# An FFT long convolution feeding an ELU MLP: batches transformed one by one instead of in pairs

## The chip, the cores and the metric

The kernel runs on one core of a Trainium2 chip. The metric is the device time of one execution in microseconds (us). TensorE (PE) does the matmuls, ScalarE (ACT) copies and activations, VectorE (DVE) and GpSimd (POOL) the elementwise work, and the SyncE queue (SP) issues nearly all DMAs.

## The reference

For four batches of 12480 positions by 128 channels, the first part is a gated long convolution, the second an MLP over all 49920 rows:

```python
h_filt = (np.maximum(pos_emb @ w1, 0.0) @ w2) * np.exp(-0.01 * pos)[:, None]
u = x * v
y = irfft(rfft(u, 2S) * rfft(h_filt, 2S)[None])[:, :S, :]    # causal convolution
a = (x * y).reshape(B * S, D)
h = a @ w_in                                                   # 128 -> 2048
g = np.where(h > 0.0, h, np.exp(np.minimum(h, 0.0)) - 1.0)     # ELU
return g @ w_out                                               # 2048 -> 128
```

## The kernel before

The sequence of one batch is laid out as 2 halves (w) x 104 rows x 60 columns (n). The convolution is done by a two-stage transform. Stage 1 (`stage1`) loads x and v, multiplies them (`gate`, on POOL), splits the product into a high and a low part (`split`), multiplies by 104x104 matrices (tiles aps) and stores the result to DRAM (`a_d`). Stage 2 (`stage2`) loads 104 slices k, multiplies each by a 120x120 matrix from a table (`forward`, tiles xps), multiplies by the filter's spectrum on DVE (tiles p), adds on POOL, transforms back (`inverse`, tiles bps) and stores to DRAM (`b_d`). Every product is three matmuls of high and low parts (`mm3`), save those in plain 32-bit.

The MLP (`Mlp.go`) works in blocks of 416 rows. One block loads `b_d` and x, does the last inverse matmuls (`conv_out`, tiles yps), gates, transposes (`transp`), and then takes 8 steps: in each, `up_proj` does six matmuls of 416 columns (tiles fps), ACT computes the exponential (n), DVE the ELU (g), POOL a rounding cast (g_h), DVE the low part (g_l), and `down_proj`, three steps later, six matmuls more (tiles ops).

Batches go in pairs: a tile holds 2 columns n by 2 batches. The order is written out by hand:

1. Stage 1 of pair 0 alone, with the filter's MLP and its transform (class `Filter`: tiles pt, rp, hps, Hps) and the unpacking of the 64-bit weights between its steps, one filter step for each of its 30 groups.
2. Stage 2 of pair 0 alone. Here each k also makes the filter's spectrum (`spectrum`, tiles fps from hl) and stores it to `f_d`.
3. The MLP over pair 0 (60 blocks, 480 steps). After each step the generator of pair 1's transforms (`side`, from `fft1`) is advanced by 0.92 of a step on average; 8 of its steps run before the MLP. Pair 1's stage 2 reads `f_d`.
4. The MLP over pair 1 (480 steps) with no transforms beside it and a third PSUM buffer pair for up_proj (`psf2`).

Pair 0's transforms keep 32-bit tiles in DRAM and split them after loading (`split_a`, `split_b`); pair 1's write the high and low parts already split. Each engine takes its instructions in this written order.

Of the kernel before, what the change touches and what calls it, by code (L numbers as in the profile page):

```python
# [19 lines left out]
TC = 5 * N2 + RI  # L20
G = 2
NG = N2 // G
HB = 2
CH = HB * D
NT = G * HB * N1
TG = 2
DFF = 2048
# [3 lines left out]
NBK = 2 * NG  # L31
FWD = ((0, 1), (2, 0))
# [4 lines left out]
def fftconv_gate_elu_mlp_kernel(ctx: ExitStack, tc: tile.TileContext, x, v, pos_emb, w1, w2,  # L37
# [21 lines left out]

    a_d = [dram.tile([N1, h + 1, 2, N2, 2, CH], F32, name=f"a_d{h}") for h in range(2)]  # L60
    b_d = [dram.tile([N1, 2, h + 1, 2, N2, CH], F32, name=f"b_d{h}") for h in range(2)]
# [17 lines left out]
    def stage1(st, h, ps_pool, ps_tag, first, eng_gate):  # L79
        b0 = h * HB  # L80
        xv = st.enter_context(tc.tile_pool(name=f"xv{h}", bufs=3 if first else 2))
        up = st.enter_context(tc.tile_pool(name=f"up{h}", bufs=2))
        ap = st.enter_context(tc.tile_pool(name=f"ap{h}", bufs=5 if first else 3))
        ld, us = {}, {}

        def load(g):
            if g >= NG:
                return
            xt = xv.tile([N1, 2, HB, G, D], F32, tag="xt", name="xt")
            vt = xv.tile([N1, 2, HB, G, D], F32, tag="vt", name="vt")  # L90
            for w in range(2):
                nc.sync.dma_start(out=xt[:, w], in_=xq[:, w, b0:b0 + HB, g * G:(g + 1) * G, :])
                nc.sync.dma_start(out=vt[:, w], in_=vq[:, w, b0:b0 + HB, g * G:(g + 1) * G, :])
            ld[g] = (xt, vt)

        def gate(g):
            if g >= NG:
                return
            xt, vt = ld[g]
            e = nc.vector if first and g < 2 else eng_gate  # L100
            e.tensor_tensor(out=vt, in0=xt, in1=vt, op=ALU.mult)  # L101

        def split(g):
# [3 lines left out]
            u_h = up.tile([N1, 2, HB, G, D], F32R, tag="u_h", name="u_h")  # L107
            u_l = up.tile([N1, 2, HB, G, D], F32R, tag="u_l", name="u_l")
# [4 lines left out]
        if first:  # L113
            filt = Filter(st)
        for g in range(3 if first else 2):
            if first:
                filt.load(g)
            load(g)
            if first:
                filt.load_w(g)  # L120
        gate(0)
        gate(1)
        if first:
            for q in range(3):
                filt.step(0, q)
        split(0)
        stores = []

        def store():
            if stores:  # L130
                g, r, t = stores.pop()
                nc.sync.dma_start(out=a_d[h][:, :, r, g * G:(g + 1) * G].rearrange("k z n w c -> k z (n w c)"),
                                  in_=t.bitcast(F32).rearrange("k z n w c -> k z (n w c)"))

        for g in range(NG):
            gate(g + 2) if first else None
            u_h, u_l = us.pop(g)
            for i in range(4):
                r, w = divmod(i, 2)
                f = FWD[w][r]  # L140
                if w == 0:
                    a_sb = ap.tile([N1, 1 + h, G, 2, CH], F32R if h else F32, tag="a_sb", name="a_sb")
                ps = ps_pool.tile([N1, 512], F32, tag=ps_tag, name="aps")
                mm3(ps, dft_h[:, f, :], dft_l[:, f, :], u_h[:, w], u_l[:, w])
                dst = [a_sb[:, z, :, w, :].rearrange("p n (b d) -> p b n d", b=HB) for z in range(1 + h)]
                src = ps.rearrange("p (b n d) -> p b n d", b=HB, n=G)
                if first and w == 0:
                    nc.vector.tensor_copy(out=dst[0], in_=src)
                else:
                    copy(dst[0], src)  # L150
                if not first:
                    nc.vector.tensor_tensor(out=dst[1], in0=src, in1=dst[0], op=ALU.subtract)
                if first and i < 3:
                    filt.step(g + 1, i)
# [4 lines left out]
                if i == 0:  # L159
                    if first:  # L160
                        filt.load(g + 3)
                        filt.load_w(g + 3)
                    load(g + (3 if first else 2))
                if i == 1:
                    split(g + 1)
                    if first:
                        filt.split_w(g - 1)
# [3 lines left out]
            if first:  # L171
                filt.transform(g)
                filt.weights(g)
# [5 lines left out]
    class Filter:  # L179
# [3 lines left out]
        def __init__(self, st):  # L183
            c1 = st.enter_context(tc.tile_pool(name="c1", bufs=1))
            self.pp = st.enter_context(tc.tile_pool(name="pp", bufs=3))
# [12 lines left out]
        def load(self, g):  # L198
            if g >= NG:
                return  # L200
            p = self.pp.tile([N1, 2, G, 64], F32, tag="pos", name="pos")
            nc.sync.dma_start(out=p, in_=posq[:, :, g * G:(g + 1) * G, :])
            self.pos[g] = p

        def step(self, g, q):
            if g >= NG:
                return
            hp, psh = self.hp, self.psh
            if q == 0:
                p = self.pos.pop(g)  # L210
                pt = psh.tile([64, 2 * G, N1], F32, tag="h", name="pt")
                for n in range(2 * G):
                    nc.tensor.transpose(out=pt[:, n, :], in_=p[:, n // G, n % G, :], identity=id_sb[:N1, :N1])
                pt_sb = hp.tile([64, 2 * G, N1], F32, tag="pt_sb", name="pt_sb")
                copy(pt_sb, pt)
                self.t[g] = pt_sb
            elif q == 1:
                rp = psh.tile([64, 2 * G, N1], F32, tag="h", name="rp")
                nc.tensor.matmul(out=rp, lhsT=self.w1, rhs=self.t[g], start=True, stop=True)
                r_sb = hp.tile([64, 2 * G, N1], F32, tag="r_sb", name="r_sb")  # L220
                nc.scalar.activation(out=r_sb, in_=rp, func=ACTF.Relu)
                self.t[g] = r_sb
            elif q == 2:
                r_sb = self.t.pop(g)
                hps = psh.tile([N1, 2, G, D], F32, tag="h", name="hps")
                for n in range(2 * G):
                    nc.tensor.matmul(out=hps[:, n // G, n % G, :], lhsT=r_sb[:, n, :], rhs=self.w2,
                                     start=True, stop=True)
                h_sb = hp.tile([N1, 2, G, D], F32, tag="h_sb", name="h_sb")
# [508 lines left out]
```

## Time and profile before

| what | value |
|---|---|
| time, median of 3 runs | 3669.15 us (3665.28 to 3671.24) |
| the profiled execution: time, span | 3675.88 us, 3674.1 us |
| mean granted TensorE clock | 0.967 of full speed |
| busy: PE, DVE, ACT, POOL | 94%, 84%, 66%, 63% of the span |
| DMA: bytes, mean rate | 525.90 MB, 143 GB/s |
| chain that ended last: PE, DVE, DMA | 67%, 10%, 10% of the span |

Busy shares are unions over the span; matmuls overlap one another, so a PE at 94% is not one that could not take more. The four stages have different limits and have to be read one by one.

### The profile page before, as it was taken

How to read it: one execution, taken by the hardware profiler on the slowest of the kernel's cores; microseconds unless marked ns; L12 is line 12 of the kernel's file. 1: busy time of each engine (PE TensorE's matmuls, PEld its weight loads, DVE VectorE, ACT ScalarE, POOL GpSimd, SP SyncE). 2: the span in 40 equal slices, each digit the busy share in tenths (PEclk: the TensorE clock that was granted, in tenths of full speed). 3: DMA queues.
4: the chain of work that ended last, by engine and by line, in shares of the span. 5: the costliest groups of instructions: out<-in, count | busy, mean ns of one | idle time of the engine just before them, and what ended most of it. 6: DMA issues, size and time to landing. Idle time of an engine off the chain costs nothing.

```text
span 3674.1 us, 50190 instructions
## 1 busy us (share of the span) xinstructions
PE 3439.7 (94%) x16780; PEld 2981.2 (81%) x16780; DVE 3098.9 (84%) x3803; ACT 2419.5 (66%) x3238; POOL 2320.9 (63%) x1508
## 2 busy tenths in 40 slices
PE   7887888779998999999999999989999999999999
PEld 4565555468887888888888888879999999999998
DVE  5566999879998998998898898968888888888887
ACT  3344554467886666666676666757777777777776
POOL 2233888747776777777677677645555565655655
PEclk8688999989999999999999999999999999999999
DMA  5687888766676455555555455332222222222220
GB/s 178 194 276 231 255 254 255 230 192 204 209 211 188 134 160 169 158 156 153 156 165 168 135 167 170 107 77 70 57 66 61 60 67 57 70 57 69 58 64 19
DMA packets 352784, 525.90 MB, mean 143 GB/s; under 512 B 24678, under 2 KB 220358, under 8 KB 352526
## 3 DMA queue, kind: packets, MB, share of 16 engines
q1 hardware_dynamic: 352105, 522.52, 48.9%
q8 instruction: 134, 2.20, 0.2%
q14 instruction: 124, 1.02, 0.1%
q10 hardware_dynamic: 421, 0.16, 0.0%
HBM read 318.12 MB, written 204.47 MB: 142 GB/s over the span
## 4 chain that ended last, share of the span: by engine, by line
PE 67%; DVE 10%; DMA 10%; issue 4%; SPq 3%; ACT 3%; POOL 2%; POOLq 0%; DVEq 0%; ACTq 0%
PE ops L52 9%; PE ops L51 9%; PE fps L51 8%; PE fps L52 8%; PE fps L53 8%; PE ops L53 8%; DVE g_l L571 3%; PE bps L428 3%; DMA h_d<-hsb 2%; DMA al<-a_d 2%; PE otp L593 1%; PE yps L52 1%; PE yps L51 1%; PE yps L53 1%; PE xps L51 1%
## 5 line engine op out<-in xcount | busy, mean ns | idle before, releaser
L565 POOL CAST g_h<-g 128x832 fp32r<-128x832 f32 x960 | 1308.9, 1365 | 963.7 <-DVE g L562 947.4
L562 DVE SCALAR_TENSOR_TENSOR g<-n,fps 128x832 f32<-128x832 f32 x960 | 975.6, 1016 | 332.8 <-ACT n L556 328.5
L555 ACT ACTIVATE n<-fps 128x832 f32<-128x832 f32 x960 | 832.1, 867 | 631.4 <-PE fps L53 618.3
L571 DVE TENSOR_TENSOR g_l<-g,g_h 128x832 fp32r<-128x832 f32 x960 | 1113.9, 1160 | 7.7 <-POOL g_h L565 7.7
L556 ACT ACTIVATE n<-n 128x832 f32<-128x832 f32 x960 | 864.7, 901 | 30.5
L51 PE MATMUL fps<-t_h,wi_h 128*128 128x416 f32 x1920 | 722.9, 376 | 20.7 <-DVE g L562 19.5
L52 PE MATMUL ops<-g_l,wo_h 128*128 128x416 f32 x1920 | 685.1, 357 | 28.8 <-DVE g_l L571 28.4
L51 PE MATMUL ops<-g_h,wo_h 128*128 128x416 f32 x1920 | 683.1, 356 | 8.0 <-ACT o_sb L56 0.7
L52 PE MATMUL fps<-t_l,wi_h 128*128 128x416 f32 x1920 | 676.3, 352 | 0.0
L53 PE MATMUL fps<-t_h,wi_l 128*128 128x416 f32 x1920 | 675.8, 352 | 0.0
L53 PE MATMUL ops<-g_h,wo_l 128*128 128x416 f32 x1920 | 675.4, 352 | 0.0
L408 POOL TENSOR_TENSOR p<-p 120x768 f32<-120x768 f32 x206 | 478.1, 2321 | 92.2 <-DVE p L400 48.6
L51 PEld LDWEIGHTS fps<-t_h,wi_h 128*128 128x128 f32 x1920 | 363.2, 189 | 62.5 <-DVE g L562 24.5
L52 PEld LDWEIGHTS ops<-g_l,wo_h 128*128 128x128 f32 x1920 | 362.2, 189 | 61.0 <-DVE g_l L571 57.5
L52 PEld LDWEIGHTS fps<-t_l,wi_h 128*128 128x128 f32 x1920 | 364.9, 190 | 31.2 <-issue 14.2
L51 PEld LDWEIGHTS ops<-g_h,wo_h 128*128 128x128 f32 x1920 | 361.7, 188 | 32.4 <-issue 28.3
L53 PEld LDWEIGHTS fps<-t_h,wi_l 128*128 128x128 f32 x1920 | 362.5, 189 | 3.5
L53 PEld LDWEIGHTS ops<-g_h,wo_l 128*128 128x128 f32 x1920 | 361.8, 188 | 4.0
L101 POOL TENSOR_TENSOR vt<-xt,vt 104x1024 f32<-104x1024 f32 x58 | 145.7, 2512 | 247.6 <-DMA vt<-in_v_dram 216.5
L395 DVE TENSOR_TENSOR p<-xps,f 120x512 f32<-120x512 f32 x416 | 282.4, 679 | 10.2 <-PE xps L53 6.3
L428 PE MATMUL bps<-p,t 120*120 120x512 f32 x416 | 218.1, 605 | 43.8 <-POOL p L409 42.2
L409 POOL TENSOR_TENSOR p<-p 120x256 f32<-120x256 f32 x206 | 235.1, 1141 | 16.1
(100 smaller groups left out, 4428.2 us busy)
## 6 DMA issues: line engine op xcount, KB each, us to landing
a_d<-a_sb SPq DMA_DIRECT2D x60, 832.0 KB
al<-a_d SPq DMA_DIRECT2D x104, 480.0 KB
b_d<-b_sb SPq DMA_DIRECT2D x104, 480.0 KB
b<-b_d SPq DMA_DIRECT2D x60, 832.0 KB
t<-in_tab_dram SPq DMA_DIRECT2D x104, 393.8 KB
xt<-in_x_dram SPq DMA_DIRECT2D x120, 208.0 KB
vt<-in_v_dram SPq DMA_DIRECT2D x120, 208.0 KB
a_d<-a_sb SPq DMA_DIRECT2D x60, 416.0 KB
```

The costliest lines, as they stand in the source:

```text
L51: nc.tensor.matmul(out=ps, lhsT=hi, rhs=bh, start=start, stop=False)
L52: nc.tensor.matmul(out=ps, lhsT=hi, rhs=bl, start=False, stop=False)
L53: nc.tensor.matmul(out=ps, lhsT=lo, rhs=bh, start=False, stop=stop)
L395: nc.vector.tensor_tensor(out=p[:, :2], in0=ps[:, :CH].rearrange("p (u b d) -> p u b d", u=1, b=HB).to_broadcast([RI, 2, HB, D]), in1=f[:, ...
L408: e.tensor_tensor(out=q, in0=q, in1=p, op=ALU.add)
L409: e.tensor_tensor(out=q[:, 1], in0=q[:, 1], in1=q[:, 2], op=ALU.add)
L428: nc.tensor.matmul(out=ps, lhsT=t[:, o, 5 * N2:], rhs=y[:, :2], start=True, stop=True)
L555: nc.scalar.activation(out=n, in_=ps[:, :, :NT], func=ACTF.Relu, scale=-1.0)
L556: nc.scalar.activation(out=n, in_=n, func=ACTF.Exp, scale=-1.0)
L562: nc.vector.scalar_tensor_tensor(out=g, in0=n, scalar=-1.0, in1=ps[:, :, :NT], op0=ALU.add, op1=ALU.max)
L565: nc.gpsimd.tensor_copy(out=g_h, in_=g)
L571: nc.vector.tensor_tensor(out=g_l, in0=g, in1=g_h, op=ALU.subtract)
```

## The change

Batches are transformed one at a time. Stage 1 takes groups of 4 columns n of one batch where it took 2 columns of 2 batches, stage 2 takes two slices k of one batch where it took one slice of two. Only batch 0 is transformed ahead of the MLP. The MLP is one loop over 120 blocks; its side work in quarter p is the transforms of batch p + 1, advanced by 1.04 of a step at each MLP step, and in the last quarter there is none. The filter keeps its groups of 2 columns, so each of its 30 steps now goes beside half a group of stage 1. The stage 2 table loses its duplicated columns (420 to 300); ahead of the MLP, POOL copies the columns that `spectrum` needs twice into a tile td.

The core of the diff:

```diff
-TC = 5 * N2 + RI
-G = 2
+TC = 3 * N2 + RI
+G = 4
+GF = 2
+SHARE = 1.04
...  stage1: the filter's steps, two for each group g of four
-                if first and i < 3:
-                    filt.step(g + 1, i)
+                if first:
+                    q = 2 * g + r
+                    filt.step(q + 1, 2 * w)
                 ps = ps_pool.tile([N1, 512], F32, tag=ps_tag, name="aps")
                 mm3(ps, dft_h[:, f, :], dft_l[:, f, :], u_h[:, w], u_l[:, w])
...
+                    if w == 0:
+                        filt.step(q + 1, 1)
+                        filt.load(q + 4)
+                        filt.load_w(q + 4)
+                    else:
+                        filt.transform(q)
+                        filt.weights(q)
+                        filt.split_w(q - 1)
...  stage2
-        d = 4 if first else 3
+        d = 3 if first else 2
...  split_t
-            th = tp.tile([RI, TG, 4 * N2], F32R, tag="th", name="th")
-            tl = tp.tile([RI, TG, 4 * N2], F32R, tag="tl", name="tl")
+            th = tp.tile([RI, TG, 3 * N2], F32R, tag="th", name="th")
+            tl = tp.tile([RI, TG, 3 * N2], F32R, tag="tl", name="tl")
...
+            if first:
+                td = tp.tile([RI, TG, 2, 2, N2], F32, tag="td", name="td")
+                for r in range(2):
+                    v = t[:, :, (1 + r) * N2:(2 + r) * N2].rearrange("p o (u n) -> p o u n", u=1)
+                    nc.gpsimd.tensor_copy(out=td[:, :, r], in_=v.to_broadcast([RI, TG, 2, N2]))
...  forward
-            ps = ps_pool.tile([RI, 2 * CH], F32, tag=ps_tag, name="xps")
-            mm3(ps, th[:, o, c:c + RI], tl[:, o, c:c + RI], a_h, a_l)
+            ps = ps_pool.tile([RI, TG, 2, D], F32, tag=ps_tag, name="xps")
+            for o in range(TG):
+                mm3(ps[:, o].rearrange("p w d -> p (w d)"), th[:, o, c:c + RI], tl[:, o, c:c + RI], a_h[:, o], a_l[:, o])
...  stage2's loop: inverse one turn behind, where it was two
-            split_a(k + 2)
-            inverse(k - 2)
-            yield
+            inverse(g - 1)
             yield
...  Mlp
-            blocks = [(w, n) for w in range(2) for n in range(NG)]
+            blocks = [(b, w, n) for b in range(NB) for w in range(2) for n in range(NG)]
+            ALL = len(blocks)
...
+                if s == (NB - 1) * per:
+                    psf2 = alone()
...
-                while side is not None and done < (s + 1) * share:
+                p, q = divmod(s, per)
+                if q == 0:
+                    done = 0
+                while p in side and done < (q + 1) * SHARE:
                     done += 1
-                    if next(side, None) is END:
-                        side = None
+                    if next(side[p], None) is END:
+                        del side[p]
...
-                    if c == 0:
-                        split_b(j + 2)
                     if c == 1:
                         conv_out(j + 1)
                         load(j + 3)
+                    if c == 2:
+                        split_b(j + 2)
...
-            run = mlp.run(sx, 0)
-            next(run)
-            side = fft1(psx)
-            for _ in range(8):
-                next(side)
-            side = run.send((side, 0.92))
+        side = {p: fft(p + 1, psx) for p in range(NB - 1)}
+        mlp.run(side, alone)
```

On PE in stage 1 ahead of the MLP, one turn of the filter stood among twelve matmuls of 512 columns (pt, rp, hps are the filter's MLP, aps is stage 1; the transform Hps follows):

```order
L213 MATMUL pt<-id_sb,pos 64x104 x4
L51 MATMUL aps<-u_h,dft_h 104x512
L52 MATMUL aps<-u_l,dft_h 104x512
L53 MATMUL aps<-u_h,dft_l 104x512
L219 MATMUL rp<-pt_sb,w_sb 64x416
L51 MATMUL aps<-u_h,dft_h 104x512
L52 MATMUL aps<-u_l,dft_h 104x512
L53 MATMUL aps<-u_h,dft_l 104x512
L227 MATMUL hps<-w_sb,r_sb 104x128 x4
L51 MATMUL aps<-u_h,dft_h 104x512
L52 MATMUL aps<-u_l,dft_h 104x512
L53 MATMUL aps<-u_h,dft_l 104x512
```

The same turn now, up to the first matmuls of Hps:

```order
L217 MATMUL pt<-id_sb,pos 64x104 x4
L53 MATMUL aps<-u_h,dft_h 104x512
L54 MATMUL aps<-u_l,dft_h 104x512
L55 MATMUL aps<-u_h,dft_l 104x512
L223 MATMUL rp<-pt_sb,w_sb 64x416
L231 MATMUL hps<-w_sb,r_sb 104x128 x4
L53 MATMUL aps<-u_h,dft_h 104x512
L54 MATMUL aps<-u_l,dft_h 104x512
L55 MATMUL aps<-u_h,dft_l 104x512
L53 MATMUL Hps<-h_h,dft_h 104x256
L54 MATMUL Hps<-h_l,dft_h 104x256
L55 MATMUL Hps<-h_h,dft_l 104x256
```

Two aps triples stand beside a filter turn where four stood, and rp and hps are neighbours.

On PE in stage 2 ahead of the MLP, from one inverse (bps) to the next, before (one k of two batches; fps is the spectrum, xps the forward transform):

```order
L428 MATMUL bps<-p,t 120x512
L380 MATMUL fps<-hl,t 120x256 x2
L51 MATMUL xps<-a_h,th 120x512
L52 MATMUL xps<-a_l,th 120x512
L53 MATMUL xps<-a_h,tl 120x512
L51 MATMUL xps<-a_h,th 120x512
L52 MATMUL xps<-a_l,th 120x512
L53 MATMUL xps<-a_h,tl 120x512
```

Now (two k of one batch), the first half; six more xps rows follow before the next bps:

```order
L439 MATMUL bps<-p,t 120x256 x2
L395 MATMUL fps<-hl,td 120x256 x4
L53 MATMUL xps<-a_h,th 120x256
L54 MATMUL xps<-a_l,th 120x256
L55 MATMUL xps<-a_h,tl 120x256
L53 MATMUL xps<-a_h,th 120x256
L54 MATMUL xps<-a_l,th 120x256
L55 MATMUL xps<-a_h,tl 120x256
```

One turn keeps the columns of forward and inverse and has twice the spectrum; there are 52 turns where there were 104.

On SP at the start of the MLP, before (xt and vt are loads of pair 1's stage 1, a_d_58 its stores; b and x are the loads of the MLP's first blocks):

```order
L93 DMA vt<-in_v_dram 104x2x256
L132 DMA a_d_58<-a_sb 208x1x1024 x2
L92 DMA xt<-in_x_dram 104x2x256
L93 DMA vt<-in_v_dram 104x2x256
L92 DMA xt<-in_x_dram 104x2x256
L93 DMA vt<-in_v_dram 104x2x256
L132 DMA a_d_58<-a_sb 208x1x1024
L499 DMA b_6834<-b_d_59 104x2x512
L501 DMA x_6835<-in_x_dram 104x2x256
```

Now, from the last stores of stage 2 on:

```order
L429 DMA b_d_61<-b_sb 120x2x256 x2
L504 DMA b_5089<-b_d_61 104x8x128
L505 DMA x_5088<-in_x_dram 104x512
L504 DMA b_5094<-b_d_61 104x8x128
L505 DMA x_5093<-in_x_dram 104x512
L504 DMA b_5121<-b_d_61 104x8x128
L505 DMA x_5120<-in_x_dram 104x512
L93 DMA xt<-in_x_dram 104x2x512
L94 DMA vt<-in_v_dram 104x2x512
```

The MLP's loads come first and the next batch's transform starts behind them, inside the loop.

## Rows read from the trace of the kernel before

**Rows 1.** Busy time by stage: stretch, length, PE, PEld, DVE, ACT, POOL, PEclk, DMA share, GB/s

```profile
0.00:334.00 334.00, 264.81 (x1140) 180.22 (x1140) 188.45 (x344) 131.60 (x230) 83.49 (x48) 0.81 0.69 222
334.00:717.00 383.00, 338.75 (x1243) 221.71 (x1244) 364.04 (x569) 192.82 (x360) 318.99 (x205) 1.00 0.79 248
717.00:766.00 49.00, 19.00 (x40) 8.80 (x38) 16.63 (x20) 11.81 (x17) 11.26 (x6) 0.56 0.66 201
766.00:1175.00 409.00, 394.37 (x1979) 349.63 (x1980) 393.32 (x409) 331.42 (x440) 294.18 (x161) 0.99 0.67 199
1175.00:1196.00 21.00, 5.55 (x20) 4.17 (x19) 5.66 (x8) 4.15 (x6) 5.34 (x4) 0.63 0.78 199
1196.00:2402.00 1206.00, 1169.74 (x5731) 1032.56 (x5730) 1099.06 (x1371) 817.22 (x1044) 865.84 (x604) 0.99 0.53 152
2402.00:2424.00 22.00, 10.74 (x43) 7.46 (x42) 5.63 (x6) 3.79 (x6) 3.61 (x3) 0.74 0.45 119
2424.00:3661.00 1237.00, 1229.75 (x6558) 1171.26 (x6559) 1021.13 (x1074) 923.16 (x1136) 734.42 (x478) 1.00 0.25 61
```

**Rows 2.** Tile fps: count, ns min/median/max, first and last start in us

```profile
L51 PE MATMUL fps<-t_h,wi_h x1920: 346/353/757, 766.4 to 3661.3; 128*128 128x416 f32 x192
```

**Rows 3.** Timeline of ACT in stage 1 with weights: start, us, idle before and releaser

```profile
128.14 0.60 ACT L56 ACTIVATE hsb<-Hps 104x512 f32<-104x512 f32 x1 [4.97 <-DMA h_d<-hsb]
...
141.14 0.60 ACT L56 ACTIVATE hsb<-Hps 104x512 f32<-104x512 f32 x1 [4.65 <-DMA h_d<-hsb]
```

**Rows 4.** Timeline of PE late in stage 1, one filter turn without weights

```profile
269.50 0.91 PE L219 MATMUL rp<-pt_sb,w_sb 64*64 64x416 f32 x2 [1.32 <-ACT pt_sb L56]
...
273.03 0.28 PE L51 MATMUL Hps<-h_h,dft_h 104*104 104x256 f32 x1
273.15 0.28 PE L52 MATMUL Hps<-h_l,dft_h 104*104 104x256 f32 x1
...
277.06 0.91 PE L219 MATMUL rp<-pt_sb,w_sb 64*64 64x416 f32 x2 [0.69 <-ACT pt_sb L56]
```

**Rows 5.** Timeline of PE in stage 2 ahead of the MLP, one k

```profile
606.05 1.02 PE L428 MATMUL bps<-p,t 120*120 120x512 f32 x2
606.91 1.03 PE L380 MATMUL fps<-hl,t 120*120 120x256 f32 x4
607.59 0.59 PE L51 MATMUL xps<-a_h,th 120*120 120x512 f32 x1
...
609.18 1.02 PE L428 MATMUL bps<-p,t 120*120 120x512 f32 x2
```

**Rows 6.** Groups of instructions from 334 to 717 us: busy us, mean ns, idle before

```profile
L408 POOL TENSOR_TENSOR p<-p 120x768 f32<-120x768 f32 x103 | 221.7, 2153 | 85.8 <-DVE p L400 48.6 <-DMA al<-a_d 35.3 <-PE bps L428 1.7
L395 DVE TENSOR_TENSOR p<-xps,f 120x512 f32<-120x512 f32 x207 | 140.3, 678 | 5.6 <-PE xps L53 1.7 <-ACT f L56 1.3 <-issue 1.0
...
L409 POOL TENSOR_TENSOR p<-p 120x256 f32<-120x256 f32 x102 | 100.5, 985 | 8.0
L369 DVE TENSOR_TENSOR a_l<-al,a_h 120x512 fp32r<-120x512 f32 x104 | 93.1, 896 | 15.8 <-ACT a_h L56 15.6
L341 DVE TENSOR_TENSOR tl<-t,th 120x480 fp32r<-120x480 f32 x51 | 87.4, 1713 | 0.3 <-ACT th L56 0.2
L400 DVE TENSOR_TENSOR p<-xps,f 120x256 f32<-120x256 f32 x207 | 84.5, 408 | 0.0
```

**Rows 7.** The page's costliest groups: POOL's cast

```profile
L565 POOL CAST g_h<-g 128x832 fp32r<-128x832 f32 x960 | 1308.9, 1365 | 963.7 <-DVE g L562 947.4
```

**Rows 8.** Timeline of PE where pair 1 goes from stage 1 to stage 2

```profile
1192.44 0.75 PE L51 MATMUL xps<-al,th 120*120 120x512 f32 x1 [15.45 <-DMA f<-f_d]
```

**Rows 9.** Timeline of PE at the first matmul of pair 1, and of the MLP

```profile
732.18 0.76 PE L51 MATMUL aps<-u_h,dft_h 104*104 104x512 f32 x1 [11.22 <-ACT u_h L56]
...
760.32 0.75 PE L51 MATMUL yps<-b_h,dft_h 104*104 104x512 f32 x1 [13.20 <-ACT b_h L56]
```

**Rows 10.** Groups of instructions from 1196 to 2402 us: the split of the table

```profile
L341 DVE TENSOR_TENSOR tl<-t,th 120x480 fp32r<-120x480 f32 x50 | 47.5, 950 | 0.0
```

More of the change, by code (lines that the diff above doesn't have):

```diff
@@ L131, in store @@
                 g, r, t = stores.pop()
-                nc.sync.dma_start(out=a_d[h][:, :, r, g * G:(g + 1) * G].rearrange("k z n w c -> k z (n w c)"),
-                                  in_=t.bitcast(F32).rearrange("k z n w c -> k z (n w c)"))
+                nc.sync.dma_start(out=a_d[h][:, r, g * G:(g + 1) * G].rearrange("k n z c -> k (n z c)"),
+                                  in_=t.bitcast(F32).rearrange("k n z w d -> k (n z w d)"))
+        if first:
+            filt = Filter(st)
+            for g in range(4):
+                filt.load(g)
+                if g < 3:
+                    load(g)
+                filt.load_w(g)
+            gate(0)
+            gate(1)
+            for q in range(3):
+                filt.step(0, q)
+        else:
+            load(0)
+            load(1)
+            gate(0)
+            gate(1)
+        split(0)
         for g in range(NG):
-            gate(g + 2) if first else None
+            if first:
+                gate(g + 2)
             u_h, u_l = us.pop(g)
@@ L427, in inverse @@
                               **({"bufs": 2} if first else {}))
-            nc.tensor.matmul(out=ps, lhsT=t[:, o, 5 * N2:], rhs=y[:, :2], start=True, stop=True)
-            b = bp.tile([RI, 2, 1 + h, CH], F32R if h else F32, tag="b", name="b_sb")
-            src = ps.rearrange("p (w c) -> p w c", w=2)
-            copy(b[:, :, 0], src)
+            for o in range(TG):
+                nc.tensor.matmul(out=ps[:, o], lhsT=t[:, o, 3 * N2:], rhs=y[:, o, :2], start=True, stop=True)
+            b = bp.tile([RI, TG, 2, Z, D], F32 if first else F32R, tag="b", name="b_sb")
@@ L441, in stage2 @@
         split_a(0)
-        split_a(1)
-        for k in range(N1):
-            g, o = divmod(k, TG)
-            if o == 0:
-                load_t(g + 3)
-                split_t(g + 1)
-            store()
-            load_a(k + d)
-            spectrum(k)
-            if first:
-                fs_t = fs[k]
-            forward(k, 0)
+        for g in range(NK):
+            load_t(g + 3)
+            split_t(g + 1)
+            store()
+            load_a(g + d)
+            spectrum(g)
+            forward(g, 0)
@@ L454, in stage2 @@
             yield
-            forward(k, 1)
-            if first:
-                nc.sync.dma_start(out=f_d[k], in_=fs_t[:N2])
+            split_a(g + 1)
+            forward(g, 1)
             yield
-            split_a(k + 2)
-            inverse(k - 2)
+            inverse(g - 1)
             yield
-        for k in range(N1 - 2, N1):
-            inverse(k)
-            store()
-            yield
+        store()
+        inverse(NK - 1)
+        yield
         store()
@@ L609, in go @@
             transp(0)
-            steps = [(j, c) for j in range(NBK) for c in range(NP)]
+            load(2)
+            steps = [(j, c) for j in range(ALL) for c in range(NP)]
+            per = NBK * NP
             done = 0
```

376 lines of the change are left out of this document (174 added, 202 removed).

## The prediction

> **What bounds the kernel now.** I read the busy times by stage first [rows 1], because the page's 94% for PE is a mean over stages with different limits. The reader is to see five stretches. Stage 1 of pair 0 with the filter takes 334 us; PE is busy 265 of them at a granted clock of 0.81, a mix of its two levels (1.2 and 2.4 GHz), and no engine is full. Stage 2 of pair 0 takes 383 us at the upper level; DVE is busy 364 of them (95%), PE 88%, POOL 83%, so DVE is the limit. The start of the MLP costs 49 us with PE busy 19. From 766 to 2424 us the MLP runs over pair 0 with pair 1's transforms beside it: PE is busy 96 to 97%, DVE 96% and then 91%. From 2424 on the MLP runs alone, with PE at 99% and DVE at 83%. The first MLP matmul starts at 766.4 and the last step at 3661.3 [rows 2].
>
> Two stretches of the mixed part stand out: 21 us from 1175, where pair 1 passes from stage 1 to stage 2 and PE waits 15.45 us for the first loads [rows 1, 8], and 22 us from 2402, the change from one pair to the next [rows 1].
>
> So PE's work is nearly the whole time from 766 on, and the part ahead of it is where PE's work is poorly covered. The change moves one batch's transforms from ahead of the MLP to beside it. It removes work from a stretch with gaps and adds it to one that is nearly full; the sum is the difference.
>
> **Stage 1 ahead of the MLP (334 us now).** One filter turn with weights took 13.0 us, by two successive hsb copies; each waited almost 5 us for the store of an earlier hsb to land [rows 3]. One without weights took 7.56 us [rows 4]. 16 turns of the one and 14 of the other make 314 us, which leaves 20 for lead-in and lead-out. The filter's 30 turns stay. Each loses two of four aps triples; six matmuls of 512 columns take 1.59 us in [rows 5], so a triple is 0.8 us and the loss 1.6 us. One of the lost triples stood between rp and hps and covered ACT's relu, which PE now waits for: about 0.85 us, an ACT copy of 0.60 [rows 3] and two handovers. On every second turn ACT's copy u_h, longer than that, stands ahead of pt_sb: 0.5 us on the mean. So 7.56 - 1.6 + 0.85 + 0.5 = 7.3, taken as 7.4. A turn with weights lies between half of before (6.5, if transfers alone set it, since half the rows of x, v and a_d go with it) and 13.0 - 1.6 = 11.4. I take 8.2, near the other kind, with 0.8 for DVE's unpacking, because more buffers for the weights let the loads run further ahead. Sum: 20 + 16 x 8.2 + 14 x 7.4 = 255 us; ends 207 (turns of 6.5 and 5.96) and 306 (11.4 and 7.4).
>
> **Stage 2 ahead of the MLP (383 us now, 104 turns).** There will be 52 turns. DVE's work in one: two multiplies of each size 2 x (0.678 + 0.408), a_l 0.896, tl at three quarters of its columns 1.713 x 0.75 = 1.28, together 4.35 us [rows 6]. PE's: 3.13 us as now plus one more spectrum of 0.68, 3.81 us [rows 5]. POOL's: adds of 2.15 + 0.99, and two copies td that no row shows; at 240 elements each they cost 0.39 by the rate of the cast [rows 7] or 0.92 by that of the short add [rows 6], so POOL is at 3.9 to 5.0 us. The inverse stood two turns behind and now stands one, so a chain closes over two turns: adds 3.14, bps 0.86, both spectra 1.36, half of xps 0.8, multiplies 1.09, a_l 0.90, multiplies 1.09, with handovers 9.7 us. That is 4.9 us a turn, above DVE's sum, and 255 us in all. Ends: 226 (DVE's sum) and 307 (one us of copies more in each turn).
>
> **Start of the MLP (49 us now).** Before, PE waited 11.22 us for pair 1's first product and 13.20 us for the MLP's first load, because eight steps of transforms and their transfers went ahead [rows 9]. Now the MLP's loads come first on SP. Store landing, load, split and conv_out remain: I take 25 us, between 20 and today's 49. The first MLP matmul is then at 255 + 255 + 25 = 535 us.
>
> **The three mixed quarters.** Before: 2424 - 766 = 1658 us for two batches, 829 each. Of this the passage between stages (15.5 us of idle PE) and the change of pair (22 us, PE busy 10.7, some of it at the lower clock: about 14 lost) came once for two batches [rows 1, 8]; without them it is 829 - 14.75 = 814. A passage now comes in every quarter: 15.5 plus 2.5 for the clock of 0.63 around it, 18 us. The change of pair goes, since loads run on across batches. But each quarter starts a new stage 1: loads, gate, u_h, in order on SP, POOL, ACT; PE waited 11.22 us for that [rows 9], and one step's matmuls cover some 2 to 3, so 8 us. The table is split for every batch: 26 more tl of 0.950 x 0.75 = 0.71 us [rows 10], 18 us of DVE; DVE stood below PE there, so I count 4. The density of 1.04 for 0.92 costs nothing by itself, as about 31 steps of each quarter then run alone; PE's share of both is the same work. Sum: 814 + 18 + 8 + 4 = 844 us, 2532 for three. The lower end is PE's work: 240 steps of 2.58, 60 triples of 0.8, 52 turns of 1.59 + 0.86, together 795; the upper 867, with the table and the start in full.
>
> **The last quarter.** 1237 us for 479 steps is 2.58 each [rows 1, 2]; 240 steps and a tail of 10 are 630 us.
>
> Sum of spans: 535 + 2532 + 630 = 3697 us, against 3674.1. The profiled execution's time was 1.8 above its span and 6.7 above the median of the runs, so the forecast is 3692 us: **0.6% slower**. The gain ahead of the MLP (766 - 535 = 231) is a little less than what the third mixed quarter costs over one alone (844 - 620 = 224) plus 15 us on each of the other two.
>
> **Rivals.**
>
> *A. The part ahead of the MLP halves better (faster).* It speaks for it that no engine was full in stage 1 and that the long wait there is for transfers, of which a large part goes; against it that the filter's chain keeps its length with half the cover. With turns of 7.0 and 6.4, 222 us, stage 2 at 4.4, 229 us, the start 25 and quarters of 838, the span is 476 + 2514 + 630 = 3620, the time 3615. The point that decides is the first MLP matmul: with my quarters the kernel is as fast as before if it starts at 512 us, faster if earlier.
>
> *B. Transfers late in stage 2 (slower).* load_t waits on SP for the inverse at the end of the turn, and the loads behind it come a turn ahead where they came three k ahead; the table and the spectrum are loaded for each batch. For it: the DMA share of 0.79 in the 383 us stage and PE's 15.45 us for one such load [rows 1, 8]. Against: 0.53 in the mixed stage 2. One us in each of 156 turns gives 3692 + 156 = 3848.
>
> *C. The td copies hold up DVE.* tl took 1.713 us ahead of the MLP, where POOL is 83% busy, and 0.950 beside the MLP, where POOL is 72% busy [rows 1, 6, 10], so the two disturb each other. If each turn pays one us, 52 us come on top: 3744. The Trainium skill states this as a rule (SBUF — State Buffer, section "Who interferes with whom"): a DVE instruction with both inputs in SBUF contends with a GpSimd instruction that reads SBUF. The two means of tl agree with it.
>
> *D. Loading weights is the limit.* forward has twice as many loads, 1248 more. The load unit is busy 1171 of 1237 us in the last stretch for 6559 loads, 0.18 us each [rows 1]; if these cannot hide, 223 us come on top: 3915. Against: Hps's matmuls of 256 columns, each with its own weights, start 0.12 us apart [rows 4], half of a 512-column one (0.265 in [rows 5]), so the loads hide. The Trainium skill counts the load unit's busy share as a good measure of the distance to the limit (Trainium Kernel Development and Optimization, section "Performance Expectations"); the 0.12 us here speaks against taking it so for this change.
>
> **How the numbers follow.** Chances: forecast 0.47, A 0.32, B 0.09, C 0.09, D 0.03. What a measurement can tell from no change is about 0.2%, 7 us to either side of 3669. The forecast's own range, 3660 to 3725, has 0.34 of its chance above that bound, 0.10 within and 0.03 below; A has 0.28 below and 0.04 within; B, C and D are above. So faster 0.31, same 0.14, slower 0.55. The unknown terms (50 us to either side in each of two stages ahead of the MLP, 25 to 50 a quarter) do not all go one way; 3625 to 3755 leaves out the far part of A, B and D.
>
> **What would show it.** Right: the first MLP matmul near 535 us; stage 2 turns of about 4.9 us with bps waiting for POOL's adds; three stops of 15 to 20 us of PE at the passages, one in each quarter; stops of about 8 us at steps 240 and 480; no stop at step 720 and 2.58 us a step after it; mixed quarters of about 844 us. Wrong: a first MLP matmul before 512 us, quarters of 815 or less (then PE hides the passages), or al and f named as what PE waits for in every turn of stage 2.

## The result and the profile after

The changed kernel takes 3637.84 us (median of four runs, 3631.71 to 3646.31) against 3670.19 us for the kernel before beside it: a ratio of 0.9916, 95% interval 0.9894 to 0.9938. It is 0.8% faster where 0.6% slower was forecast: the time lies inside the 3625 to 3755 us that were stated, the direction does not agree. The profiled execution spans 3644.5 us. First its busy time by stage, with the columns of [rows 1]:

```profile
20.00:150.00 130.00, 112.19 (x482) 83.19 (x482) 88.69 (x207) 50.38 (x96) 59.37 (x22) 0.76 0.62 188
150.00:284.00 134.00, 108.19 (x460) 78.46 (x461) 58.54 (x89) 47.68 (x84) 20.09 (x12) 0.70 0.52 147
284.00:534.00 250.00, 223.54 (x1240) 191.61 (x1239) 219.74 (x308) 133.03 (x255) 196.53 (x202) 0.98 0.84 255
534.00:553.00 19.00, 6.40 (x18) 3.48 (x18) 5.85 (x9) 3.46 (x5) 0.21 (x1) 0.69 0.50 136
553.00:1394.00 841.00, 789.58 (x4289) 732.05 (x4290) 770.96 (x927) 585.46 (x775) 592.06 (x383) 0.98 0.66 188
1394.00:2205.00 811.00, 784.52 (x4316) 738.43 (x4315) 736.92 (x930) 564.61 (x751) 516.98 (x358) 0.99 0.74 209
2205.00:3015.00 810.00, 783.27 (x4314) 737.32 (x4314) 734.78 (x930) 564.36 (x750) 520.52 (x358) 0.99 0.73 208
3015.00:3644.00 629.00, 620.16 (x3312) 590.51 (x3310) 515.27 (x542) 464.35 (x572) 370.26 (x242) 1.00 0.24 57
```

The reader is to lay these beside the terms of the sum. Stage 1 ends at 284 (255 forecast), stage 2 takes 250 (255), the start 19 (25), so the MLP begins at 553 and not at 535: the part ahead was worse than forecast. The first mixed quarter takes 841 (844), the last 629 (630). The second and third take 811 and 810 where 844 stood; these two differences of 34 us are together more than the whole error of the sum (3697 against 3644.5). The odd thing is that the first quarter and the later ones, which run the same steps, differ by 30 us. DVE is at 92% in the first and 91% in the others, but over a shorter time: 771 us against 737.

The groups of DVE and POOL in a stretch of stage 2 within the first quarter (790 to 1280 us), then the same within the second (1630 to 2090 us):

```profile
L567 DVE TENSOR_TENSOR g_l<-g,g_h 128x832 fp32r<-128x832 f32 x139 | 170.3, 1225 | 0.0
L412 DVE TENSOR_TENSOR p<-xps,f 120x512 f32<-120x512 f32 x96 | 65.2, 680 | 0.0
L347 DVE TENSOR_TENSOR tl<-t,th 120x360 fp32r<-120x360 f32 x48 | 46.1, 961 | 0.0
L515 POOL TENSOR_TENSOR b<-b,b 104x1024 fp32r<-104x1024 f32 x18 | 43.2, 2401 | 0.0
```
```profile
L567 DVE TENSOR_TENSOR g_l<-g,g_h 128x832 fp32r<-128x832 f32 x136 | 153.0, 1125 | 0.0
L412 DVE TENSOR_TENSOR p<-xps,f 120x512 f32<-120x512 f32 x95 | 64.9, 683 | 0.1
L347 DVE TENSOR_TENSOR tl<-t,th 120x360 fp32r<-120x360 f32 x47 | 27.4, 583 | 0.0
```

In the first quarter alone POOL makes batch 0's low part (b<-b,b, 2.40 us each), and there g_l is 100 ns and tl 378 ns longer, while p, which reads PSUM, is not. Over this window that makes 139 x 0.10 + 48 x 0.38 = 32 us more of DVE, where POOL's b_l takes 43 us. In the kernel before, every mixed block is of pair 0 and has such a b_l. This was theory T1 of the runs below: half of before's mixed stretch is too large a base for a quarter whose b arrives split.

### The profile page after: what moved, and what is told of

It is laid out like the page before. It is cut to its first block, busy times and chain, and to the rows that moved or that the text cites. A ratio compares the mean times of both kernels' runs of the same rounds, so it can differ in the third digit from the quotient of the medians.

```text
span 3644.5 us, 53113 instructions
## 1 busy us (share of the span) xinstructions
PE 3434.0 (94%) x18444; PEld 3158.4 (87%) x18444; DVE 3136.5 (86%) x3941; ACT 2418.3 (66%) x3290; POOL 2276.2 (62%) x1578
## 4 chain that ended last, share of the span: by engine, by line
PE 76%; DVE 8%; ACT 4%; DMA 4%; issue 4%; POOL 3%; SPq 0%; POOLq 0%; DVEq 0%; ACTq 0%
PE fps L53 9%; PE fps L55 9%; PE fps L54 9%; PE ops L53 9%; PE ops L54 9%; PE ops L55 8%; PE bps L439 4%; DVE g_l L567 2%; PE xps L53 2%; PE xps L54 2%; PE xps L55 2%; PE yps L53 2%; PE yps L54 2%; PE yps L55 2%; PE otp L589 1%
## 5 line engine op out<-in xcount | busy, mean ns | idle before, releaser
L561 POOL CAST g_h<-g 128x832 fp32r<-128x832 f32 x960 | 1232.5, 1286 | 1051.3 <-DVE g L558 1050.5
L567 DVE TENSOR_TENSOR g_l<-g,g_h 128x832 fp32r<-128x832 f32 x960 | 1097.7, 1143 | 9.3 <-POOL g_h L561 9.3
L421 POOL TENSOR_TENSOR p<-p 120x256 f32<-120x256 f32 x204 | 246.0, 1206 | 16.0
L439 PE MATMUL bps<-p,t 120*120 120x256 f32 x832 | 219.1, 385 | 31.5 <-POOL p L421 26.6
L347 DVE TENSOR_TENSOR tl<-t,th 120x360 fp32r<-120x360 f32 x208 | 202.1, 971 | 44.9 <-ACT th L58 31.4
```

Of the source, the lines that this page charges most:

```text
L421: e.tensor_tensor(out=q[:, :, 1], in0=q[:, :, 1], in1=q[:, :, 2], op=ALU.add)
L439: nc.tensor.matmul(out=ps[:, o], lhsT=t[:, o, 3 * N2:], rhs=y[:, o, :2], start=True, stop=True)
L561: nc.gpsimd.tensor_copy(out=g_h, in_=g)
L567: nc.vector.tensor_tensor(out=g_l, in0=g, in1=g_h, op=ALU.subtract)
```

## The experiments

### b_l, and why it costs

The first run leaves POOL's subtraction out of split_b:

```diff
                 if bt is not None:
                     copy(t[:, :, :, 0], bt)
-                    e = nc.gpsimd if j > 1 else nc.vector
-                    e.tensor_tensor(out=t[:, :, :, 1], in0=bt, in1=t[:, :, :, 0], op=ALU.subtract)
```

> The changed kernel with GpSimd's subtraction that makes batch 0's low part b_l left out (the high part is used in its place, so every matmul stays); ScalarE's copy that makes the high part stays. Its first mixed quarter took 841 us, the two later ones, whose b arrives split, 810. Theory T1 (GpSimd's b_l, both inputs in SBUF, 2.40 us, slows VectorE's g_l from 1.13 to 1.23 us and tl from 0.58 to 0.96, and VectorE then paces PE): the first quarter falls to 808 to 816, the whole from 3638 to about 3610 (0.9% less). H2 (ScalarE's copy of b_h, which stands ahead of the relu and exp of later steps and waits for the load, is what costs): no change, 838 to 843. H3 (b_l keeps GpSimd's queue busy, so that the casts g_h come late): as T1. H4 (the load of batch 0's b in 512-byte pieces is late): no change.

It took 3594.26 us (ratio to the kernel before 0.9794, 0.9771 to 0.9817). The first quarter by windows, and DVE's groups from 790 to 1280 us:

```profile
553.00:1357.60 804.60, 779.95 (x4289) 732.25 (x4290) 731.66 (x926) 584.59 (x775) 522.55 (x356) 0.98 0.70 196
```
```profile
L565 DVE TENSOR_TENSOR g_l<-g,g_h 128x832 fp32r<-128x832 f32 x146 | 164.5, 1127 | 0.0
L347 DVE TENSOR_TENSOR tl<-t,th 120x360 fp32r<-120x360 f32 x49 | 28.4, 579 | 0.0
```

805 for 841, with g_l and tl as short as in the later quarters. How DVE's delay reaches PE stands in PE's waits from 790 to 1280 us (us in total, times, longest), with b_l and then without it:

```profile
PE ops L54 <- DVE g_l L567: 11.8, 16, 1.2
PE otp L589 <- DVE t_l L540: 7.1, 10, 1.7
```
```profile
PE ops L54 <- DVE g_l L565: 1.0, 5, 0.2
```

ScalarE's copy and its load are still there, so H2 and H4 fall for this quarter. T1 and H3 (POOL's queue) are left. The second run puts fills in the subtraction's place:

```diff
-                    e.tensor_tensor(out=t[:, :, :, 1], in0=bt, in1=t[:, :, :, 0], op=ALU.subtract)
+                    for i in range(2):
+                        s = self.b0.tile([N1, 2, G, D], F32, tag="s", name="fill", bufs=1)
+                        nc.gpsimd.memset(s, 0.0)
```

> As the run without b_l, but in place of each subtraction GpSimd fills a tile of the same size with zeros twice, which nobody reads: its queue stays busy for about as long, and it reads no SBUF. T1 (VectorE is slowed while GpSimd reads two SBUF inputs): first quarter 808 to 818, g_l near 1.13 us, whole near 3610. H3 (the queue's occupation delays g_h): first quarter 830 to 841, VectorE waits for g_h before g_l as it does now, whole near 3635. If two fills take much less than 2.4 us the run does not tell them apart and a longer one is needed.

It took 3607.35 us (0.9827, 0.9812 to 0.9841), the first quarter 815. From 790 to 1280 us:

```profile
L569 DVE TENSOR_TENSOR g_l<-g,g_h 128x832 fp32r<-128x832 f32 x145 | 168.8, 1164 | 0.9 <-POOL g_h L563 0.9
L348 DVE TENSOR_TENSOR tl<-t,th 120x360 fp32r<-120x360 f32 x49 | 30.2, 616 | 0.0
L517 POOL MEMSET fill<- 104x1024 f32 x36 | 34.3, 953 | 1.0
```

Two fills hold POOL for 1.91 us a block, four fifths of b_l's time, and 26 of the 36 us stay saved: most of b_l's price is not the time that it takes in POOL's queue, and what the fills lack is the reading. DVE waited 0.9 us for g_h in all, so the queue is not it. The last 9 us are as much as g_l's remaining 37 ns over 240 steps; why it is longer beside the fills is not settled. What a subtraction on POOL does to DVE the Trainium skill states as a rule (SBUF — State Buffer, section "Who interferes with whom"): a DVE instruction with both inputs in SBUF contends with a GpSimd instruction that reads SBUF, not with one that only writes. These rows agree for tl and, less cleanly, for g_l.

The third keeps all of the computation and writes batch 0's b split, as the other batches do (b_d with two halves, VectorE's subtraction after b_sb, no split_b):

```diff
-            if not first:
+            if True:
                 nc.vector.tensor_tensor(out=b[:, :, :, 1], in0=ps, in1=b[:, :, :, 0], op=ALU.subtract)
```

> The changed kernel with batch 0's b written already split by its stage 2 ahead of the MLP, as the other batches do: VectorE makes the low part there from PSUM, the store is twice as large, and ScalarE's copy and GpSimd's subtraction beside the MLP go. All of the computation stays. T1 and H3: first quarter 808 to 816 (30 less). In stage 2 ahead of the MLP VectorE gains 52 instructions of about 0.62 us (its subtraction for the other batches); if VectorE paces it, 32 us come on top (250 becomes 282) and the whole stays at 3638; if the chain of adds paces it, as bps waits for GpSimd's adds in 48 of 52 turns, it grows by 0 to 10 and the whole is near 3612. I take 3622. H2 and H4 expect the first quarter to fall too, so this run does not tell those apart; the run without b_l does.

It took 3617.78 us (0.9857, 0.984 to 0.9873): the first quarter 812, and 281 us for stage 2 and the start together where they took 270, near the 10 of a chain that POOL's adds pace and far from the 32 of a full VectorE.

### What before's mixed stretch held

The same cut in the kernel before (b_l left out, b_h used twice), and then a second cut beside it: each load of the table issued after the inverse that frees its buffer.

> The kernel before with GpSimd's (for the first two blocks VectorE's) subtraction b_l of pair 0 left out, the high part used in its place. If T1 is what the forecast missed, half of the 1658 us of before's mixed stretch is too large a base for a quarter whose b arrives split: without b_l the mixed stretch should fall by about 50 to 60 us (to 1600 to 1610), the whole from 3670 to about 3615. If H2 holds (the copy of b_h or its wait for the load), it stays at 1650 to 1660 and the whole at 3665 to 3670. If the gain comes from the change's own order (one load of a turn earlier, blocks of one batch), it also stays.

```diff
             if o == 0:
-                load_t(g + 3)
                 split_t(g + 1)
...
             inverse(k - 2)
+            if o == 1:
+                load_t(g + 3)
```

> The kernel before without b_l (as in the run that left out b_l of pair 0) and, beside that, with each load of the table issued after the inverse of its turn's second k instead of at the turn's start, so that SyncE's queue no longer stands up to 24 us at that load with the loads of b behind it. Without b_l the mixed stretch still had 15 us of PE gaps of 1 to 4.5 us that ended when ScalarE's copy b_h got its late load. Theory: these are a second part of what half of before's mixed stretch holds and a later quarter of the changed kernel does not: the mixed stretch falls from 1617 to 1597 to 1605 and ScalarE's wait of 50 us for b goes. Rival: the loads are late because the DMA engines are busy, not because SyncE is held: 1612 to 1620 and the wait stays.

They took 3635.33 us (0.9904, 0.9889 to 0.9919) and 3579.25 us (0.9747, 0.9724 to 0.9769). The mixed stretch, from the first MLP matmul to that of pair 1, in the kernel before, without b_l, and with both cuts:

```profile
766.40:2424.10 1657.70, 1580.38 (x7768) 1393.81 (x7768) 1503.63 (x1793) 1156.34 (x1493) 1168.96 (x770) 0.98 0.57 164
```
```profile
762.20:2379.10 1616.90, 1562.72 (x7769) 1393.11 (x7769) 1451.95 (x1794) 1154.10 (x1493) 1013.95 (x712) 0.99 0.58 168
```
```profile
740.90:2327.60 1586.70, 1553.37 (x7769) 1392.10 (x7769) 1451.90 (x1794) 1155.59 (x1493) 1021.62 (x712) 0.99 0.60 171
```

PE's count of matmuls stays. The time beside its busy time shrinks (77 us, 54, 33), and its busy time by 18 and 9. b_l was worth 41 us (less than the 50 to 60 expected), and the loads 30 (more than the 12 to 20); with the loads moved, the MLP also starts 21 us earlier. How the second part came about is in the waits of ACT, then of SyncE's queue, from 1200 to 2250 us without b_l, and in those of PE from 762 to 2380 us:

```profile
ACT b_h L56 <- DMA b<-b_d: 50.5, 14, 7.6
```
```profile
SPq L331 <- PE bps L428: 526.1, 41, 24.0
```
```profile
PE fps L51 <- DVE g L559: 16.3, 8, 4.5
```

SyncE stood up to 24 us at a load of the table whose buffer the inverse at the end of the turn's second k set free. The load of b was queued behind it, ACT's in-order copy b_h waited up to 7.6 us for that, and the relu and exp of the steps behind the copy came late, so PE stood at fps. With both cuts the row for b_h is gone from ACT's waits and that for fps from PE's. These stops are 16 of the 30 us; the rest is not placed.

In the changed kernel the same edit was run alone:

> The changed kernel with each load of the table issued after the inverse of its turn, not at its start (the edit that took 30 us off the mixed stretch of the kernel before without b_l, and 15 us off the part ahead of its MLP). Theory: in the changed kernel this wait costs nothing beside the MLP, since PE shows no gap of over 2 us in stage 2 of a quarter and no copy on ScalarE stands behind the load of b: quarters stay at 841, 810, 810. If it does cost, the quarters fall to 800 to 805. Stage 2 ahead of the MLP (250 us) may lose up to 10 us. Whole: 3625 to 3640.

3628.67 us (0.9894, 0.987 to 0.9917), quarters of 840, 805 and 805. The first agrees with the theory; the two later ones are at the edge of the alternative. The seven traces that leave the later quarters as the change made them have 806 to 811 there, so the gain is some 4 us each. From the first spectrum matmul to the MLP the time stayed at 269 us (270 in the changed kernel). Its trace is 23 us shorter than that of the changed kernel, and 12 of these are stage 1, which the edit does not touch (see below). SyncE's longest wait at that load had become 13.0 us in the second quarter by the change itself (24 before), since the inverse now stands in the third step of the transforms from its load and not in the sixth:

```profile
SPq L336 <- PE bps L439: 232.9, 42, 13.0
```

### Stage 1: the clock

Turns of the changed kernel's filter at PE, late in stage 1 (start, us):

```profile
240.64 1.64 PE L223 MATMUL rp<-pt_sb,w_sb 64*64 64x416 f32 x2
242.88 2.03 PE L231 MATMUL hps<-w_sb,r_sb 64*104 64x128 f32 x8 [0.60 <-ACT r_sb L225]
...
250.91 0.99 PE L223 MATMUL rp<-pt_sb,w_sb 64*64 64x416 f32 x2
252.51 1.12 PE L231 MATMUL hps<-w_sb,r_sb 64*104 64x128 f32 x8 [0.60 <-ACT r_sb L225]
...
257.94 0.91 PE L223 MATMUL rp<-pt_sb,w_sb 64*64 64x416 f32 x2 [0.98 <-ACT pt_sb L58]
259.45 1.12 PE L231 MATMUL hps<-w_sb,r_sb 64*104 64x128 f32 x8 [0.60 <-ACT r_sb L225]
...
263.94 0.91 PE L223 MATMUL rp<-pt_sb,w_sb 64*64 64x416 f32 x2
```

The wait for relu is 0.60 us (0.85 forecast), but the same eight matmuls take 2.03 us and, ten us later, 1.12: PE goes between its two levels. The turn from the first rp to the second takes 10.3 us, the last one, at the upper level and with the same wait, 6.0.

Seven traces hold this stage as the change made it: that of the changed kernel, and those of the runs without b_l, with the fills, with b written split, with the loads moved and of the two runs with pauses. It ended anywhere from 271.8 to 283.6 us in them, earlier where the granted clock was higher. The two ends, the changed kernel and the one with the loads moved, from 0 to the first spectrum matmul:

```profile
0.00:283.60 283.60, 226.16 (x961) 164.61 (x961) 152.60 (x300) 102.97 (x186) 79.67 (x37) 0.75 0.59 170
```
```profile
0.00:271.80 271.80, 211.62 (x961) 155.46 (x961) 150.86 (x300) 102.53 (x186) 80.19 (x37) 0.80 0.61 177
```

Three runs separate the wait from the level: hps moved behind the second triple, each triple issued twice, and both.

```diff
                 if first:
                     q = 2 * g + r
-                    filt.step(q + 1, 2 * w)
+                    if w == 0:
+                        filt.step(q + 1, 0)
...
                     else:
+                        filt.step(q + 1, 2)
                         filt.transform(q)
```
```diff
-                mm3(ps, dft_h[:, f, :], dft_l[:, f, :], u_h[:, w], u_l[:, w])
+                for i2 in range(2 if first else 1):
+                    mm3(ps, dft_h[:, f, :], dft_l[:, f, :], u_h[:, w], u_l[:, w])
```

> The changed kernel with the filter's third matmul hps issued after the second aps triple of its turn instead of ahead of it, so that a triple stands again between rp and hps. Stage 1 ahead of the MLP took 284 us (first spectrum matmul at 283.6) with a wait of 0.60 us for relu in each of 29 turns and a granted clock of 0.70 to 0.76. If the exposed waits alone cost: 284 falls by 29 x 0.6 = 17 to about 266. If the low clock is the larger part and the gap is what lowers it, it falls further, to about 240. If PE's work at that clock is the limit and the wait only moves elsewhere (to Hps or to pt_sb): 278 to 286. Whole: 3638 less the same; I take 3620.

> The changed kernel with each aps triple of stage 1 ahead of the MLP issued twice into the same PSUM tile (the second overwrites the first), which gives PE back the columns per turn that it had before. At the clock of 0.70 that would add 60 triples of about 1.1 us, 66 us: stage 1 from 284 to 350. If the change lost the upper clock level because a turn now has less work for PE, the doubled triples raise the clock and the stage stays at 270 to 295 with PE's busy share above 0.9. I expect the second, about 290.

> The changed kernel with both edits of stage 1: hps behind the second triple, and each aps triple issued twice. Moving hps alone gave two times, 3582 (mean granted clock 0.985) and 3634 to 3652 (0.962 to 0.972); doubling alone gave 3630 to 3633 with the clock at 0.92 in the stage. Theory: the stage is bistable in its clock, and the doubled triples hold PE at the upper level: all runs agree, with the first spectrum matmul of stage 2 at 220 to 245 us and the whole at 3585 to 3605, although PE has 60 more triples. Rival: at the upper level the turn is set by the chain over ScalarE and VectorE or by transfers, and the extra triples only fill it: 265 to 275 as with doubling alone, whole 3625 to 3635.

Moving hps gave two kinds of runs of one kernel: 3582 us twice, at a mean granted clock of 0.985, and four of 3635 to 3653 at 0.962 to 0.967 (0.972 in the profiled one, 3640, whose stage 1 ends at 280). Its comparison (0.9803, 0.9748 to 0.9858) is therefore unclear, and its trace, of one of the longer runs, is not compared here. Doubling took 3632.56 us (0.9891, 0.9873 to 0.991), stage 1 ending at 274; both together 3603.35 us (0.982, 0.9805 to 0.9834), ending at 244, all four runs within 4.4 us. From 150 to 240 us in the changed kernel, doubled, and with both:

```profile
150.00:240.00 90.00, 79.32 (x320) 58.17 (x320) 42.63 (x66) 33.11 (x58) 18.66 (x8) 0.66 0.52 146
```
```profile
150.00:240.00 90.00, 81.65 (x429) 58.90 (x428) 47.27 (x63) 35.45 (x62) 15.74 (x7) 0.92 0.56 157
```
```profile
150.00:240.00 90.00, 81.57 (x461) 57.34 (x460) 45.23 (x56) 37.57 (x65) 7.15 (x3) 0.98 0.58 169
```

In 90 us PE gets through 320, 429 and 461 matmuls with about the same busy time; the clock is the difference. 180 matmuls that nobody needs cost nothing: 274 us lies within the 272 to 284 of the seven traces without them, where 66 us more were expected at the clock of 0.70. With the gap closed as well the stage took 244, below all of them. So the low clock is the larger part of the 29 us missed: a turn at the upper level (6.0 us, its wait included) is shorter than the 7.4 forecast, one at the lower level (10.3) longer. Beside doubled triples, closing the gap takes off 30 us (274 to 244) and not its own 29 x 0.6 = 17, with the clock going from 0.92 to 0.98: where hps stands counts for the clock too. What decides between the levels is not shown. Extra matmuls are not needed for the upper one: if the rest of the kernel took the same time, the two runs of 3582 us, of which no trace was kept, ended stage 1 near 222 us (an estimate: 280 less the 58 between 3640 and 3582).

### Pauses at the passages

The transforms of a batch give back control after their first loads, so that MLP steps run alone until these land:

```diff
             load(0)
             load(1)
+            yield HOLD1
             gate(0)
             gate(1)
         split(0)
+        if not first:
+            yield HOLD2
...
+        if not first:
+            yield HOLD3
         split_t(0)
...
+                    elif r:
+                        done += r * SHARE
```

> The changed kernel in which a batch's transforms pause after they have issued their first loads: 3 MLP steps after the loads of x and v, 2 after the first split, 7 after the first loads of stage 2; the MLP's own steps run on meanwhile, and the same work is done in the end. In the changed kernel PE stood at each passage (17.6 us longer than a usual step) and at each quarter's start (13 us, and 6 in the step after). Theory: both are loads seen from PE's queue, which the pauses cover: 3 x 17 and 3 x 8 to 15 us go, 3638 becomes 3555 to 3585. Rival: the loads are late whenever they are issued, because SyncE's queue is held by earlier waits, and the stall only moves: 3625 to 3640.

3618.22 us (0.9861, 0.9843 to 0.9879), quarters 841, 804, 802: both expectations missed, because the loops around stage1 and stage2 did not pass the lengths on, and each pause lasted one step. Passed on:

> The pauses as they were meant: in the first run with pauses their lengths were lost on the way, so that each lasted one MLP step (quarters of 804 and 802 for 811 and 810). Now 4 steps after the loads of x and v, 2 after the first split, 7 after the first loads of stage 2; the transforms run at 1.12 of their steps per MLP step in place of 1.04, so that they end in time. Theory: the loads are merely seen from PE's queue; PE's gaps of 6.2 us at a quarter's start and 11.2 us at the passage go, the quarters become 790 to 796, the first about 826, the whole about 3590. Rival: the later part of the stage is limited by something else at the higher density (VectorE), and gives it back: 800 to 805, whole 3615 to 3625.

3608.51 us (0.9827, 0.9809 to 0.9845), quarters 829, 801.5, 803: the later quarters are the rival's, the whole lies between the two. The passage is cured (its step, 17.6 us in the second quarter, takes 5.9), the quarter's start is not: one step takes 9.6 us there. ACT and POOL:

```profile
1390.81 1.06 ACT L61 ACTIVATE u_h<-vt 104x1024 fp32r<-104x1024 f32 x1 [4.40 <-POOL vt L105]
```
```profile
1388.44 4.64 POOL L105 TENSOR_TENSOR vt<-xt,vt 104x1024 f32<-104x1024 f32 x2
```

u_h was queued right behind the gate it needs, and with it every relu and exp of the MLP behind it on ACT. That is not the limit by density that the rival named. The last run adds a pause between gate and split and puts the gains together:

> What the runs point to, put together, with all of the computation: batch 0's b written split by its stage 2 (first quarter 841 to 812, part ahead 11 longer), hps behind the second triple and each aps triple of stage 1 ahead of the MLP issued twice (first MLP matmul 553 to 513), the table's loads issued after the inverse (5 from each later quarter), and the pauses, now with one more of 3 steps between the gate and the split, since in the run with pauses ScalarE's u_h still stood 4.4 us for GpSimd's gate (quarters 810 to 800; without that stall 795). If the parts add: 524 ahead of the MLP, quarters of 797, 795, 795, a last of 630, 3541 in all and 3543 for the time, 2.6% below the changed kernel and 3.5% below the kernel before. If VectorE or the loads give back part of it, as the pauses at 1.12 steps per MLP step did: 3555 to 3575.

3549.82 us (0.9671, 0.9658 to 0.9685), 3.3% below the kernel before. By stage:

```profile
0.00:245.00 245.00, 213.62 (x1140) 147.00 (x1140) 155.12 (x300) 104.60 (x186) 79.65 (x37) 0.98 0.66 197
245.00:527.00 282.00, 232.07 (x1258) 196.89 (x1258) 228.75 (x366) 134.86 (x259) 190.34 (x202) 0.95 0.89 282
527.00:1324.00 797.00, 783.43 (x4290) 731.48 (x4291) 746.06 (x927) 561.14 (x747) 514.50 (x356) 0.99 0.77 214
1324.00:2120.00 796.00, 782.81 (x4312) 732.53 (x4311) 749.04 (x930) 562.44 (x749) 515.67 (x357) 1.00 0.77 212
```

The parts add to within 7 us of the 3543 expected, and a quarter now holds 13 us beside PE's busy time. The transforms ran at 1.14 of their steps per MLP step here, so the density was not what held the run before.

## Why the prediction was wrong, point by point

- **The step that failed: "without them it is 829 - 14.75 = 814", the base of all three mixed quarters.** It took out of before's mixed stretch what comes once for two batches, and carried everything else into every quarter. Two things in it do not pass on: b_l (41 us of 1658) and the copy b_h behind a held load of b (30 us with the loads moved, 16 of them seen as PE's stops). With both cut the stretch is 1587, or 793.4 a batch, and the prediction's own sum on that base, 793.4 - 14.75 + 18 + 8 + 4, is 809; measured were 811 and 810, and 805 with the loads moved there too. Half of the 71 us stood in the forecast of each of three quarters, and in the kernel 36 us stood in one. The two later quarters together came out 67 us shorter than forecast; a part ahead of the MLP that was 18 us longer hid some of it. That later batches arrive split stands in the code (b_d has two halves for b > 0, and split_b then does nothing); the base was not cleared of it. The prediction's own row bears its mark: tl took 0.950 us in [rows 10], and 0.669 in the same kernel without b_l (1176 to 2303 us).
- **The first quarter, 841 measured for 844, was right for another reason, by luck.** Its b_l cost 36 us there (841 to 805), about what b_l (20.5) and the held loads (15) together had put into the base. Here a copy of b waited for its load 1.5 us in all.
- **Passages and starts.** The passage's step took 17.57 us where its neighbours take 2.98, 14.6 in excess (18 forecast); PE waited 11.23 us for f, as in [rows 8]. A start took 13.18 and 6.26 in two steps, 13.5 in excess (8 forecast), with 6.21 us for u_h, as in [rows 9]. The pauses of the last run remove both: from 1324 to 2120 us PE waits 1.8 us at xps and not at all at aps. So they were what they were taken for. The prediction named quarters of 815 or less as a sign that PE hides the passages; such quarters came, and PE did not hide them.
- **The table's split, 4 us a quarter**, was not measured apart. A tl took 0.583 us in the second quarter where 0.71 was taken, so 26 more are 15 us of DVE and not 18; the sum of 809 leaves little room for more than the 4. (The upper end of 867 for a quarter does not follow from its terms: 844, 14 more for the table and 3 for the start make 861.)
- **Stage 1, 284 measured for 255: a mis-sized term.** The turns were costed at the mix of clocks that [rows 4] and [rows 1] showed, and the lost triples as saved time. Over the stage the granted clock fell from 0.81 to 0.75 (0.80 in the best of seven traces, 272 us); a turn takes 8.7 us, not 8.2 and 7.4. Held at the upper level, the stage takes 244 with twice the triples.
- **Stage 2, 250 measured for 255: right**, with bps waiting 48 times for POOL's second add, as forecast. Inside, errors offset: tl took 1.81 us, not 1.28, beside POOL; the adds 1.84 and 0.90, not 2.15 and 0.99; a copy td 0.63, between the bounds of 0.39 and 0.92.
- **Start (19 measured for 25) and last quarter (629 for 630): right.** No stop at step 720.
- **The rivals.** A named the right side for a wrong reason: it needed an MLP start before 512 us, and at 553 the kernel was faster all the same. B's load of the table behind the inverse was worth some 4 us in each of the two later quarters, by moving it, and not 52. C's contention is real, but its price lay with b_l; td was not taken out, and in stage 2, where tl took 1.81 us, the time was no longer than forecast. D: in the later quarters PE's busy time agrees with the work counted for it (785 for 795), so loading weights did not bind.

## What to carry to other kernels

When a stretch of the profile is scaled to a new arrangement, list what runs in it by tile and ask of each whether the new stretch has it; a mean rate carries the special cases of the stretch with it. An instruction on an idle engine, or a load held in a queue, can cost through the engine that it disturbs: look for an instruction of the same form whose mean differs between two stretches. Where PE has gaps, look at the granted clock before counting removed matmuls as time saved.

## What the runs showed of the hardware

- The same matmuls of stage 1 ran at either of PE's levels from turn to turn (hps 2.03 and 1.12 us), and one unchanged kernel (hps moved) took 3582 us in some runs and 3635 to 3653 in others, with the mean granted clock at 0.985 and 0.962 to 0.972.
- More matmuls did not make a stage longer: with 60 extra triples it ended at 274 us, at a granted clock of 0.92; without them at 272 to 284 us in seven traces, at 0.75 to 0.80.
- POOL's subtraction of two SBUF tiles (2.40 us) lengthened DVE's tl from 583 to 961 ns on the mean; a fill of the same tile, twice, only to 616. DVE's p, with one input in PSUM, stayed at 680 ns beside either.
